# A causal convolution, a Fourier mix and an MLP on one core: the order of GpSimd's preparations, and the shape and order of the first input transfers

## The chip, the cores and the metric

The kernel runs on one core of a Trainium2 chip. A core has five instruction queues that run beside each other and wait for one another by semaphores: TensorE (PE, matrix products into PSUM), VectorE (DVE), ScalarE (ACT), GpSimd (POOL) and SyncE (SP), which here only issues DMAs. Each queue works through its instructions in order. Sixteen DMA engines move data between the off-chip memory (DRAM) and the on-chip memory (SBUF). The metric is the time of one execution on the device in microseconds, lower is better.

## What is computed

For 8 sequences of 4224 tokens with 192 features, in float32:

```python
# x: (8, 4224, 192), weight: (8 heads, 7 taps), group = 24 features a head
w = softmax(weight, axis=-1)
x = sum over k of w[h, k] * x_padded[b, s + k, head h]     # causal, 7 taps
X = np.fft.fft(np.fft.fft(x, axis=1), axis=2)               # over tokens, then features
u = x + np.real(X)
un = (u - mean(u)) / sqrt(var(u) + 1e-6)                    # over the features
out = u + np.maximum(un @ w_ch1, 0) @ w_ch2                 # 192 -> 768 -> 192
```

## The kernel before

**Per sequence (a "batch").** The convolution is a product with a band matrix (`conv_unit`, L419), in 6 chunks of 6 windows of 120 rows; its result is stored to a scratch `sc` in DRAM (`store_rows`, L383 and L391), with the first 1080 rows stored a second time behind the last, so that reads may run past the end. The transform over 4224 = 128 x 33 tokens starts from the scratch: partition a, column b of the input holds row 33a + 128b (modulo 4224). This input comes as 33 columns in eight pieces of four or five (`PIECES`), and each piece is split into two halves of 16 bits: `XH` by ScalarE (L530) and `XL` by VectorE (L538). `stage_a` (L555 to L564) transforms over a, `stage_b` (L581 to L592) over b, and the rest is done tile by tile.

**Per tile.** A batch has nine tiles ("steps", 72 in all): eight of 512 tokens and one of 128. For each, `load_res` fetches the convolution's rows from the scratch into `u`: two of the four groups by direct transfers from SP (L621), two by an indirect gather from GpSimd (L627). `prep` finishes the transform on PE (L678), adds it to `u` on VectorE (L696), takes mean and variance there (`mv`, L703 and L704), and then, for all tiles but the very first, works on GpSimd: a chain of six small instructions for the inverse root (`v`, `y`, `t`, L723 to L728), the normalised tile `un` (L732, four instructions), its upper 16-bit half (L746) and its lower half in two instructions (L749). The last of these is noted in the dictionary `lows` under the tile's number. `transposes` (L763) turns `hl` into `kt` with a DMA transpose from SP; `mlp_hidden` (PE L792, ACT L796 for `hh`, VectorE L797 for `hlo`) and `mlp_out` (PE L811 to L817, VectorE L823) follow, and SP stores the result.

**The order of the work.** A loop over n = 0 to 72 traces the work of several tiles interleaved: the MLP of tile n with the output of n - 1, `un` and the halves of tile n + 2 (`rest`), `prep` up to `y` of tile n + 3 (`sums`), the gathers of tile n + 5, and the convolution, input and transforms of later batches as filling. The instructions' order in each engine's queue is then chosen at build time by a scheduler with a model of the times. `tc.issue_after(ins)`, and `after(ins)` which does nothing where `ins` is missing, bind that order: what is traced in the block stands behind `ins` in the queue of `ins`'s engine. It adds an order and no wait. The second batch's input pieces (`load_x`, L489) are bound behind the transpose traced last (`turn[0]`), and share four buffers.

**The very first input.** Batch 0 has no filling before it. `load_first_x` loads its input into the two buffers that later hold `yh` and `yl`, in four ranges of columns, (0, 9), (9, 17), (17, 25) and (25, 33). Each range is loaded in four transfers of 32 partitions (L515). `WRAP` gives, for each 32 partitions, the column from which the row number passes 4224. Behind the last transfer SP loads the constants (`c16`), the taps, and the second batch's windows and rows. The gathers of tiles 0 to 3 have no `lows` to stand behind.

Of the kernel before, what the change touches and what calls it, by code (L numbers as in the profile page):

```python
# [11 lines left out]
F32 = mybir.dt.float32  # L12
# [3 lines left out]
ALU = mybir.AluOpType  # L16
# [3 lines left out]
B, S, D, HID = 8, 4224, 192, 768  # L20
# [7 lines left out]
NA, NB, NJ, ND = 128, 33, 64, 3  # L28
# [6 lines left out]
AC = 32  # L35
WRAP = (33, 25, 17, 9)
# [17 lines left out]
LNEPS = 1e-6  # L54
# [72 lines left out]
def kernel(  # L127
# [13 lines left out]
    nc = tc.nc  # L141
    PSUM = bass.MemoryType.PSUM
    cp = ctx.enter_context(tc.tile_pool(name="cp", bufs=1))
    sb = ctx.enter_context(tc.tile_pool(name="sb", bufs=2))
# [63 lines left out]
    def after(ins):  # L208
        return tc.issue_after(ins) if ins else ExitStack()
# [283 lines left out]
    def load_first_x(bt):  # L493

        halves = [
            sb.tile([NA, 17, D], F32, tag=tag, name=f"xs_0_{tag}", bufs=1)
            for tag in ("yh", "yl")
        ]

        def rows_of(b0, b1):  # L500
            h, o = (halves[0], 0) if b0 < 17 else (halves[1], 17)
            return h[:, b0 - o : b1 - o]

        loads = []
        for b0, b1 in ((0, 9), (9, 17), (17, 25), (25, 33)):
            for ch in range(NA // AC):
                r = 33 * AC * ch + 128 * b0 - (S if b0 >= WRAP[ch] else 0)
                last = r + 33 * (AC - 1) + 128 * (b1 - 1 - b0)
                loads.append((b0, last, r, ch, b0, b1))
        for _, _, r, ch, b0, b1 in sorted(loads):  # L510
            src = bass.AP(
                bt.sc.tensor, bt.sc.offset + r * D,
                [[33 * D, AC], [128 * D, b1 - b0], [1, D]],
            )
            load = nc.sync.dma_start(rows_of(b0, b1)[AC * ch : AC * (ch + 1)], src)  # L515
        for i, piece in enumerate(PIECES):
            bt.xs[i] = rows_of(*piece)
        return load.ins

    def split_x(bt, i):  # L520
        b0, b1 = PIECES[i]
# [86 lines left out]
    def load_res(bt, it, g):  # L608

        b = bt.b  # L610
        if g == 0:
            bt.u[it] = sb.tile([128, 4, D], F32, tag="u", name=f"u_{b}_{it}", bufs=8)
        to = bt.u[it][:, g]

        def fetch(part, first, *dims):
            src = bass.AP(
                bt.sc.tensor,
                bt.sc.offset + first * D,
                [[step * D, n] for step, n in dims] + [[1, D]],
            )  # L620
            nc.sync.dma_start(part, src)  # L621

        if it == Q0 or g % 2:
            col = 0 if it == Q0 else 1 + 4 * it + g
            k = b * NIT + it
            with after(lows.get(k - 3, lows.get(k - 4))):
                nc.gpsimd.indirect_dma_start(  # L627
                    to, None, bt.sc[:S],
                    bass.IndirectOffsetOnAxis(ap=rows_sb[:, col : col + 1], axis=0),
                )  # L630
            return

        c0 = CG * it
        cs = -33 if g else 33

        def block(q0, q1, base):
            fetch(
                to[CG * (q0 - 1) : CG * (q1 - 1)],
                base + cs * c0 + 128 * q0, (128, q1 - q0), (cs, CG),
            )  # L640

        cut = 1
        while 128 * cut + min(cs * c0, cs * (c0 + CG - 1)) < 0:
            cut += 1
        if cut in (2, NQ - 1):
            cut += 1
        if cut > 1:
            block(1, cut, S)
        if cut < NQ:
            block(cut, NQ, 0)  # L650
        if it == 0 and g:
            fetch(to[0::CG], S // 2 + 128, (128, NQ - 1))

    def prep(bt, it):
# [47 lines left out]
        for g in range(ng):  # L702
# [5 lines left out]
        var = mv[:, :ng, 1]  # L708
        v, t, y = (
            sb.tile([128, 4], F32, tag=n, name=f"{n}_{b}_{it}", bufs=3)[:, :ng]  # L710
            for n in ("v", "t", "y")
        )
        if b + it == 0:
            V = nc.vector
            V.tensor_scalar(v, var, LNEPS, None, op0=ALU.add)
            nc.scalar.activation(y, v, AF.Sqrt)
            V.reciprocal(y, y)
            V.scalar_tensor_tensor(t, v, -0.5, y, op0=ALU.mult, op1=ALU.mult)
            V.tensor_tensor(t, t, y, op=ALU.mult)
            V.scalar_tensor_tensor(y, t, 1.5, y, op0=ALU.add, op1=ALU.mult)  # L720
        else:
            P = nc.gpsimd
            P.tensor_scalar(v, var, LNEPS, None, op0=ALU.add)  # L723
            P.tensor_tensor(y, v, minus_half[:, :ng], op=ALU.pow)
            P.tensor_tensor(t, y, y, op=ALU.mult)
            P.tensor_tensor(t, t, v, op=ALU.mult)
            P.tensor_scalar(t, t, -0.5, 1.5, op0=ALU.mult, op1=ALU.add)
            P.tensor_tensor(y, y, t, op=ALU.mult)  # L728
        yield
        un = sb.tile([128, 4, D], F32, tag="un", name=f"un_{b}_{it}", bufs=1)  # L730
        for g in range(ng):
            (nc.vector if b + it == 0 else nc.gpsimd).tensor_scalar(  # L732
                un[:, g], u[:, g], mv[:, g, 0:1], y[:, g : g + 1],
                op0=ALU.subtract, op1=ALU.mult,
# [167 lines left out]
    turn, lows = [None], {}  # L902
    first = batches[0]
# [25 lines left out]
    for ch in range(NCH):  # L929
        for part in range(3):  # L930
# [3 lines left out]
            )  # L934
    scales(first)
    last_load = load_first_x(first)
    with tc.issue_after(last_band), tc.issue_after(first.evicted):
        W1, s1 = weights_in()
# [75 lines left out]
    for n in range(len(steps) + 1):  # L1014
        bt, it = steps[n] if n < len(steps) else (None, 0)
# [93 lines left out]
```

## Time and profile before

| | us |
|---|---|
| median of 3 runs | 1238.72 |
| lowest, highest | 1238.15, 1240.5 |
| the profiled execution's own time | 1238.39 |
| its span, first to last instruction | 1236.6 |

| engine | busy us | share of the span |
|---|---|---|
| PE, matrix products | 1171.4 | 95% |
| PE, weight loads | 928.6 | 75% |
| VectorE | 818.3 | 66% |
| ScalarE | 595.6 | 48% |
| GpSimd | 768.3 | 62% |

The profile is one execution on the chip. In its rows, "L749" is a line of the kernel, the arrow in "hl<-un" leads from the tile that is read to the tile that is written, and the bracket at the end of a timeline row gives how long the engine sat idle before that row, and what ended it. SPq and ACTq are the queues of SP and ACT when they issue a DMA. The granted clock is the share of full speed at which TensorE was let run.

### The profile page before, as it was taken

What the parts mean: (1) busy time and instruction counts of PE and PEld (TensorE: products, weight loads), DVE (VectorE), ACT (ScalarE), POOL (GpSimd) and SP (SyncE); (2) the same over time, 40 slices, a digit from 0 to 9 for tenths busy, and PEclk for the clock granted to TensorE, in tenths of its full rate; (3) what the DMA queues carried; (4) which work ended last, traced back from release to release, by engine and by line L of the source; (5) the groups of instructions that cost most, each with busy time, mean ns of one, the idle gap of its engine ahead of it and who ended that gap; (6) DMA issues with size and microseconds to landing.
All of it is one profiled execution on the core that took longest, in us unless ns stands there. A gap on an engine that the chain in (4) does not pass through costs nothing.

```text
span 1236.6 us, 30122 instructions
## 1 busy us (share of the span) xinstructions
PE 1171.4 (95%) x12236; PEld 928.6 (75%) x12236; DVE 818.3 (66%) x1871; ACT 595.6 (48%) x983; POOL 768.3 (62%) x1103
## 2 busy tenths in 40 slices
PE   5289869999999999999999999999999999999998
PEld 4178657787878777787787878787687877787776
DVE  6777655687656975478656876468965687567543
ACT  5675545365544555446543565445454455333222
POOL 0207676479637785468854796467963688667840
PEclk9599989999999999999999999999999999999999
DMA  8964985566455756377645675557754643323321
GB/s 297 271 189 115 240 125 114 128 173 185 93 123 149 186 140 140 87 181 188 144 96 138 157 194 100 123 144 185 150 99 100 164 99 90 83 63 81 81 56 42
DMA packets 238506, 170.47 MB, mean 138 GB/s; under 512 B 119512, under 2 KB 222112, under 8 KB 238368
## 3 DMA queue, kind: packets, MB, share of 16 engines
q1 hardware_dynamic: 184888, 109.95, 38.9%
q10 hardware_dynamic: 46952, 45.24, 13.4%
q0 software_dynamic: 6528, 13.38, 4.4%
q8 instruction: 95, 1.56, 0.5%
q14 instruction: 43, 0.35, 0.1%
HBM read 83.82 MB, written 58.55 MB: 115 GB/s over the span
## 4 chain that ended last, share of the span: by engine, by line
PE 85%; DVE 7%; DMA 4%; ACT 1%; issue 1%; POOL 1%; SPq 1%; DVEq 0%; ACTq 0%; POOLq 0%
PE ph L792 32%; PE po L811 10%; PE po L817 10%; PE po L814 10%; PE pa L555 6%; PE pb L581 6%; PE pq L678 6%; PE pc L419 6%; DVE XL L538 1%; DMA xs<-sc 1%; DVE yl L564 1%; DVE hlo L797 1%; DVE u L696 1%; DMA xs_yh<-sc 1%; ACT XH L530 1%
## 5 line engine op out<-in xcount | busy, mean ns | idle before, releaser
L792 PE MATMUL ph<-kt,W 128*128 128x512 f16 (+1 forms) x2160 | 494.9, 362 | 8.6 <-DVE hlo L797 7.0
L797 DVE SCALAR_TENSOR_TENSOR hlo<-ph,hh 128x512 f16<-128x512 f32 (+1 forms) x400 | 271.3, 679 | 279.0 <-ACT hh L796 271.1
L796 ACT ACTIVATE hh<-ph 128x512 f16<-128x512 f32 (+1 forms) x400 | 237.0, 593 | 432.1 <-PE ph L792 422.0
L811 PE MATMUL po<-W,hh 128*128 128x192 f16 x1584 | 386.1, 246 | 9.6 <-ACT hh L796 9.6
L814 PE MATMUL po<-W,hh 128*128 128x192 f16 x1584 | 385.6, 246 | 0.0
L817 PE MATMUL po<-W,hlo 128*128 128x192 f16 x1584 | 384.6, 246 | 0.0
L792 PEld LDWEIGHTS <-W 128*128 128x128 f16 x2160 | 192.7, 98 | 149.3 <-issue 9.1
L732 POOL TENSOR_SCALAR un<-u,mv,y 128x192 f32<-128x192 f32 x260 | 270.4, 1046 | 6.5 <-POOL y L728 0.2
L627 POOL DMA_INDIRECT u<-sc,rows_sb x136 | 145.6, 1071 | 68.1 <-DMA xs_yh<-sc 37.2
L811 PEld LDWEIGHTS <-hh 128*128 128x128 f16 x1584 | 155.4, 98 | 27.2 <-ACT hh L796 10.2
L817 PEld LDWEIGHTS <-hlo 128*128 128x128 f16 x1584 | 154.8, 98 | 22.3 <-issue 0.8
L814 PEld LDWEIGHTS <-hh 128*128 128x128 f16 x1584 | 155.0, 98 | 16.8
L723 POOL TENSOR_SCALAR v<-mv 128x4 f32<-128x4 f32 (+1 forms) x71 | 24.5, 344 | 176.9 <-DVE mv L704 147.3
L419 PE MATMUL pc<-xt,band 128*120 128x144 f32 x724 | 113.0, 295 | 13.4 <-DMA band<-line_d 11.0
L749 POOL TENSOR_TENSOR hl<-un,hl 128x512 f16<-128x512 f32 (+2 forms) x142 | 121.2, 874 | 4.0
L419 PEld LDWEIGHTS pc<-xt,band 128*120 128x120 f32 x724 | 99.9, 188 | 19.9 <-issue 10.9
L538 DVE SCALAR_TENSOR_TENSOR XL<-xs,s_x,XH 128x768 f16<-128x768 f32 (+1 forms) x56 | 94.7, 1692 | 29.3 <-ACT XH L530 29.3
L601 POOL COPY V<-V 128x96 f16<-128x96 f16 x64 | 16.8, 264 | 151.3 <-DVE V L592 151.2
L696 DVE SCALAR_TENSOR_TENSOR u<-pq,g,u 128x128 f32<-128x128 f32 (+1 forms) x328 | 102.7, 378 | 12.1 <-PE pq L678 12.1
L563 ACT ACTIVATE yh<-pa 99x512 f16<-99x512 f32 x128 | 75.9, 598 | 66.1 <-PE pa L555 61.8
L555 PE MATMUL pa<-c_sb,XH 128*128 128x128 f16 x1024 | 102.1, 220 | 0.9 <-ACT XH L530 0.9
L530 ACT ACTIVATE XH<-xs,s_x 128x768 f16<-128x768 f32 (+1 forms) x56 | 93.6, 1683 | 17.3 <-DMA xs<-sc 17.3
(135 smaller groups left out, 1551.1 us busy)
## 6 DMA issues: line engine op xcount, KB each, us to landing
out_dram<-u SPq DMA_DIRECT2D x64, 384.0 KB
xt<-in_xw_dram ACTq DMA_DIRECT2D x30, 576.0 KB
sc<-xa ACTq DMA_DIRECT2D x30, 540.0 KB
xs<-sc SPq DMA_DIRECT2D x28, 288.0 KB
u<-sc SPq DMA_DIRECT2D x72, 96.0 KB
xt<-in_xw_dram SPq DMA_DIRECT2D x10, 576.0 KB
sc<-xa SPq DMA_DIRECT2D x10, 540.0 KB
xs<-sc SPq DMA_DIRECT2D x28, 192.0 KB
```

The lines of the kernel that those rows point to most:

```text
L419: nc.tensor.matmul(pc[:WR, h - h0], band[:, h, :WR], xt[:, :, h * GRP : (h + 1) * GRP], start=True, stop=True,)
L555: nc.tensor.matmul(pa[:, i], x[:, at], F[:, l], start=(n == 0), stop=(n == 2))
L627: nc.gpsimd.indirect_dma_start(to, None, bt.sc[:S], bass.IndirectOffsetOnAxis(ap=rows_sb[:, col : col + 1], axis=0),)
L696: nc.vector.scalar_tensor_tensor(to, src, bt.g, to, op0=ALU.mult, op1=ALU.add)
L732: (nc.vector if b + it == 0 else nc.gpsimd).tensor_scalar(un[:, g], u[:, g], mv[:, g, 0:1], y[:, g : g + 1], op0=ALU.subtract, op1=ALU.mult,)
L749: lower = (nc.vector if b + it == 0 else nc.gpsimd).tensor_tensor(bl[:, :, o : o + n], un[:, :ng, f], hi[:, :, f], op=ALU.subtract)
L792: nc.tensor.matmul(ph[:, n], W1[:, w, ht * 128 : (ht + 1) * 128], kt[:, k], start=(i == 0), stop=(i == len(order) - 1),)
L796: anchor[0] = nc.scalar.activation(hh, ph, AF.Relu).ins
L797: nc.vector.scalar_tensor_tensor(hlo, ph, 0.0, hh, op0=ALU.max, op1=ALU.subtract)
L811: nc.tensor.matmul(po[:, g % 2], hh[:, ht, tk], W2[:, ht, 0], start=(ht == 0), stop=False)
L814: nc.tensor.matmul(po[:, g % 2], hh[:, ht, tk], W2[:, ht, 1], start=False, stop=False)
L817: nc.tensor.matmul(po[:, g % 2], hlo[:, ht, tk], W2[:, ht, 0], start=False, stop=(ht == 5),)
```

## The change

There are three edits. In `prep`, the first GpSimd instruction of a tile is bound behind the lower halves of the last tile whose halves have been traced. In `load_first_x`, each of the four column ranges is loaded in one transfer, or in two where the row numbers wrap inside it (one below the wrap, one above), seven in all; each is bound behind the one before. A new small GpSimd copy reads four elements of column 32 in all partitions, which the last transfers write, and the gathers that have no earlier tile to stand behind (tiles 0 to 3) are bound behind that copy.

```diff
 def load_first_x(bt):
-        loads = []
+        load = None
         for b0, b1 in ((0, 9), (9, 17), (17, 25), (25, 33)):
-            for ch in range(NA // AC):
-                r = 33 * AC * ch + 128 * b0 - (S if b0 >= WRAP[ch] else 0)
-                last = r + 33 * (AC - 1) + 128 * (b1 - 1 - b0)
-                loads.append((b0, last, r, ch, b0, b1))
-        for _, _, r, ch, b0, b1 in sorted(loads):
-            src = bass.AP(
-                bt.sc.tensor, bt.sc.offset + r * D,
-                [[33 * D, AC], [128 * D, b1 - b0], [1, D]],
-            )
-            load = nc.sync.dma_start(rows_of(b0, b1)[AC * ch : AC * (ch + 1)], src)
+            cut = next(c for c in range(5) if c == 4 or b0 >= WRAP[c])
+            for c0, c1, wrap in ((0, cut, 0), (cut, 4, S)):
+                if c0 == c1:
+                    continue
+                src = bass.AP(
+                    bt.sc.tensor,
+                    bt.sc.offset + (33 * AC * c0 + 128 * b0 - wrap) * D,
+                    [[33 * D, AC * (c1 - c0)], [128 * D, b1 - b0], [1, D]],
+                )
+                with after(load):
+                    load = nc.sync.dma_start(
+                        rows_of(b0, b1)[AC * c0 : AC * c1], src
+                    ).ins
         for i, piece in enumerate(PIECES):
             bt.xs[i] = rows_of(*piece)
-        return load.ins
+        landed = sb.tile([128, 4], F32, tag="v", name="landed", bufs=3)
+        bt.landed = nc.gpsimd.tensor_copy(landed, halves[1][:, 15, :4]).ins
+        return load
...
 def load_res(bt, it, g):
-            with after(lows.get(k - 3, lows.get(k - 4))):
+            with after(lows.get(k - 3, lows.get(k - 4, first.landed))):
                 nc.gpsimd.indirect_dma_start(
...
 def prep(bt, it):
             P = nc.gpsimd
-            P.tensor_scalar(v, var, LNEPS, None, op0=ALU.add)
+            with after(lows[max(lows)] if lows else None):
+                P.tensor_scalar(v, var, LNEPS, None, op0=ALU.add)
             P.tensor_tensor(y, v, minus_half[:, :ng], op=ALU.pow)
```

## The prediction

> **What bounds the kernel now.** I read the page first, for where TensorE (PE) is not full, then a table of busy time by stage, then PE's waits, then the queues behind the longest wait.
>
> ```profile
> span 1236.6 us, 30122 instructions
> ...
> PE   5289869999999999999999999999999999999998
> ```
>
> Each digit is the busy tenth of 30.9 us. From the seventh slice on PE is full; whatever the change does to time, it does in the first six slices, or in a hole too short for a digit. The table by stage gives the columns PE, PE's weight loads, VectorE (DVE), ScalarE (ACT) and GpSimd (POOL), then granted clock, DMA share and GB/s.
>
> ```profile
> 124.00:155.00 31.00, 26.63 (x239) 20.49 (x238) 19.03 (x41) 16.93 (x21) 19.26 (x26) 1.00 0.92 237
> 155.00:186.00 31.00, 20.56 (x206) 15.68 (x204) 16.48 (x27) 13.02 (x21) 21.96 (x24) 0.83 0.82 124
> 500.00:840.00 340.00, 340.00 (x3615) 272.99 (x3614) 227.19 (x523) 168.69 (x279) 219.68 (x317) 1.00 0.59 142
> 840.00:900.00 60.00, 56.45 (x556) 42.54 (x553) 51.47 (x105) 32.54 (x50) 52.18 (x67) 0.97 0.78 167
> ```
>
> From 500 to 840 PE is busy for all of 340 us: nothing that GpSimd does better there can be seen. Between 124 and 186 it lacks 4.4 and 10.4 us, and around 870 another 3.6. PE's waits between 60 and 190 us (total, times, longest) name the places:
>
> ```profile
> PE po L811 <- ACT hh L796: 9.6, 3, 8.7
> PE ph L792 <- DVE hlo L797: 2.9, 3, 1.1
> PE pc L419 <- ACT xa L428: 2.4, 1, 2.4
> PE ph L792 <- DMA kt<-hl: 1.7, 1, 1.7
> ```
>
> One wait of 8.7 us, for an activation, outweighs the rest. Four finer stretches around it:
>
> ```profile
> 154.00:158.00 4.00, 2.95 (x27) 2.21 (x25) 4.00 (x8) 3.74 (x6) 3.60 (x3) 1.00 0.02 4
> 158.00:162.50 4.50, 4.50 (x37) 3.04 (x35) 1.98 (x4) 0.61 (x2) 4.00 (x5) 1.00 0.59 119
> 162.50:171.25 8.75, 0.05 (x2) 0.01 (x1) 0.51 (x1) 2.13 (x3) 8.41 (x13) 0.75 1.09 225
> 171.25:177.10 5.85, 5.16 (x28) 3.35 (x29) 4.20 (x5) 2.53 (x3) 5.75 (x5) 0.50 1.17 119
> ```
>
> From 162.5 to 171.25 PE stands still, and in the next 5.85 us it has half its clock: 5.16 us of work there would be 2.6 at full clock. And from 154 to 158 the DMA engines did nothing (share 0.02), just ahead of the stretch in which everything waits for a load. GpSimd's timeline says why:
>
> ```profile
> 145.26 0.82 POOL L746 CAST hl<-un 128x768 f16<-128x768 f32 x1
> 146.07 0.19 POOL L727 TENSOR_SCALAR t<-t 128x4 f32<-128x4 f32 x1
> 154.32 1.41 POOL L723 TENSOR_SCALAR v<-mv 128x4 f32<-128x4 f32 x1 [8.05 <-DVE mv L704]
> 155.81 2.94 POOL L749 TENSOR_TENSOR hl<-un,hl 128x512 f16<-128x512 f32 x2
> ```
>
> The upper half of one tile was cast by 146.1. Its lower half (L749) needs nothing more, but it is queued behind L723, the first instruction of a later tile, and that waits 8.05 us for VectorE's variance. The lower half ends at 158.75; then SyncE (SP), ACT and the transfer follow:
>
> ```profile
> 158.78 3.66 SPq L763 DMA_TRANSPOSE kt<-hl  x1
> 162.53 2.94 SPq L489 DMA_DIRECT2D xs<-sc  x4
> ```
>
> ```profile
> 164.04 5.00 DMA xs<-sc
> ```
>
> ```profile
> 169.12 1.59 ACT L530 ACTIVATE XH<-xs,s_x 128x768 f16<-128x768 f32 x1 [10.35 <-DMA xs<-sc]
> ```
>
> The transpose waits for the lower half, the second batch's last two input pieces are queued behind the transpose, one of them lands 5.00 us after its issue, and ACT sits 10.35 us in front of it, with the hh that PE wants behind that. This chain is what the GpSimd part of the change cuts.
>
> **Part one: L723 behind the lower halves of the tile ahead.** No instruction is added; an order is. What is now queued behind the waiting L723 is the later tile's own chain, the gathers and the V copies; all of these stood behind it before too. What leaves from behind it is L746 and L749.
>
> Step by step: L749 can start at 146.1 and takes 1.8 us undisturbed (below, 850.00), so the transpose is issued near 148.0 instead of 158.78, 10.8 us sooner. The four row transfers then come up near 151.7 (its 3.66 us of issue after it), if their buffers are free. A buffer is freed by the VectorE split of the piece four earlier:
>
> ```profile
> 147.21 1.56 DVE L538 SCALAR_TENSOR_TENSOR XL<-xs,s_x,XH 128x768 f16<-128x768 f32 x1 [2.31 <-ACT XH L530]
> ...
> 151.87 1.55 DVE L538 SCALAR_TENSOR_TENSOR XL<-xs,s_x,XH 128x768 f16<-128x768 f32 x1
> ```
>
> These end at 148.8 and 153.4, so the sixth piece is bound by SP, the seventh by the buffer. With the 1.5 us from first to second transfer and 5.00 to landing, the pieces land near 158.3 and 159.5, in the stretch whose DMA share is 0.02 now. ACT's wait of 10.35 us ended at 169.12, so ACT has other work until 158.8 and the wait goes nearly whole, hh follows near 161, and PE, which stopped at 162.5, does not stop. That takes out 8.7 us, and with it the 2.6 us lost at half clock: the half clock follows the stand-still. The 1.7 us for kt is the same mechanism two tiles earlier, L723 waiting in front of L749, and goes too. Sum 13.0.
>
> What is late next: the loads now fall into a time with more DMA traffic, and the two splits (1.59 us in the row above) come earlier among ACT's and VectorE's work for the MLP. I give back 1.5 us for this, one split's length. The waits for hlo (2.9) I leave standing: they come from 1.6 us splits standing between two hlo on the same engine, which the change leaves. Part one: **-11.5 us** there.
>
> The third hole has the same form, smaller:
>
> ```profile
> 849.68 0.23 POOL L723 TENSOR_SCALAR v<-mv 128x4 f32<-128x4 f32 x1 [2.13 <-DVE mv L704]
> 850.00 1.80 POOL L749 TENSOR_TENSOR hl<-un,hl 128x512 f16<-128x512 f32 x2
> ```
>
> ```profile
> 866.61 2.29 PE L792 MATMUL ph<-kt,W 128*128 128x512 f16 x5 [3.07 <-DVE hlo L797]
> ```
>
> L749 is held 2.1 us, and the transpose, the last pieces and the segment load for the final batch follow it on SP; VectorE waits for that load with hlo behind. I credit the 2.1 us that L749 is held, out of a hole of 3.07 plus about 1 us of half clock. **-2.1 us**; bounds 0 and 4.1.
>
> Everywhere else PE is full, so the new order is worth nothing, and costs nothing while GpSimd has idle time to put it in.
>
> **Part two: the first transform input.** Sixteen transfers of 32 partitions become seven of 32 to 128, in fixed order; the eight gathers of the first four tiles move behind a new 128x4 copy that waits for the last of them. The copy itself is a quarter of a microsecond on an engine that has nothing else to do (L723, the same shape, takes 0.23).
>
> ```profile
> 45.54 6.54 ACT L530 ACTIVATE XH<-xs_yh,s_x 128x768 f16<-128x768 f32 x4 [4.45 <-DMA xs_yh<-sc]
> 51.96 6.15 ACT L530 ACTIVATE XH<-xs_yl,s_x 128x768 f16<-128x768 f32 x4
> ```
>
> ```profile
> 37.62 1.27 POOL L627 DMA_INDIRECT u<-sc,rows_sb  x1 [37.19 <-DMA xs_yh<-sc]
> ```
>
> The eight ScalarE splits run back to back from 45.54 to 58.11, so this stage is set by when the *first* piece is whole, not by the last. That piece now lies in four narrow transfers, and narrow transfers of later pieces stand between them in SP's queue. After the change it is the first transfer alone. Its price: it reads nearly all rows of the scratch, so it waits for the last store. The gather, which reads all of it, started at 37.62, so the scratch was whole by then at the latest. For the speed I compare the narrow loads with a stretch that holds wide ones:
>
> ```profile
> 37.00:43.00 6.00, 0.59 (x2) 0.50 (x2) 3.41 (x11) 2.12 (x5) 4.29 (x4) 0.50 1.14 204
> 384.50:388.00 3.50, 3.50 (x38) 3.00 (x36) 3.50 (x12) 0.60 (x1) 0.26 (x1) 1.00 1.11 329
> ```
>
> ```profile
> 382.27 3.03 SPq L489 DMA_DIRECT2D xs<-sc  x6
> ```
>
> Both have a full DMA share; 204 GB/s against 329 for the same 768-byte rows out of the same scratch. The first transfer is 9 x 128 rows of 768 bytes, 0.885 MB: 2.7 us at 329, and 2.5 us more from issue to flow (a 0.295 MB load took 5.00 in a crowd). Landing: 37.6 + 5.2 = 42.8, against 45.5 now. All 3.24 MB take 9.9 us, so the last lands near 50.0; the last pieces' splits would start near 52, so ACT stays unbroken. Gain 2.7, and since 37.6 is the latest for the stores, I take **-3 us**. Bounds: 0 (narrow speed: 4.3 us instead of 2.7 for the first piece, and 15.9 for all, hence the last at 56, which eats the gain at the other end) and 4.2 (stores whole 1.5 us before the gather). Behind this stage the split, stage A and the first tiles follow in a chain, so the gain stays on the path.
>
> [...]
>
> The gathers start near 50.3 instead of 37.6, and then take their eight issues. The first tile wants its rows here:
>
> ```profile
> 75.96 1.55 DVE L696 SCALAR_TENSOR_TENSOR u<-pq,g,u 128x192 f32<-128x192 f32 x5 [1.74 <-PE pq L678]
> ```
>
> Even 3 us sooner, that is 23 us after 50.3, for two gathers of a microsecond or so each; hidden. SP comes to what is queued behind the loads (c16, the second batch's windows) after seven issues; six take 3.03 us in the row at 382.27, so no later than now.
>
> **Sum** against the profiled execution's own 1238.39 us (span 1236.6): 1238.4 - 11.5 - 2.1 - 3.0 = 1221.8. The median of the runs shown is 1238.72, 0.3 higher; I say **1222**. About 0.2% (2.5 us) is what a measurement of this kernel can tell from no change.
>
> **Rivals.**
> Forecast, 1214 to 1229: chance 0.50.
> *One, width pays nothing:* stage A starts when it did, part one stays: 1238.4 - 13.6 = 1225. For it: the share is full in both rows, so the narrow loads are not starved of work. Against: 204 and 329. 0.15.
> *Two, the wait moves:* the last pieces land no sooner than buffers and a crowded DMA allow (share 0.92 from 124 to 155), ACT still stands in front of them for half as long, and PE stops for over 3 us, so that the half clock stays: half of 8.7 back, and 2.6. 1221.8 + 7 = 1229, to 1233. Against: the share of 0.02 between 154 and 158. 0.15.
> *Three, the change doesn't do what it says:* the order of L723 is right, but another waiting instruction (a V copy, a gather) comes to stand before L749, and only the start pays, or not that: 1235 to 1238. The instructions' order is chosen anew at build time. 0.10.
> *Four, slower:* GpSimd becomes the bound. Before, a later tile's y chain (L723 to L728) filled the gaps of the tile ahead; now tiles go one after another:
>
> ```profile
> 839.95 0.24 POOL L723 TENSOR_SCALAR v<-mv 128x4 f32<-128x4 f32 x1 [3.49 <-DVE mv L704]
> ...
> 842.56 4.00 POOL L732 TENSOR_SCALAR un<-u,mv,y 128x192 f32<-128x192 f32 x4
> ```
>
> From v to un 2.6 us, un 4.0, with the rows above cast 0.8, halves 1.8 and two gathers 2.5: 11.7 us a tile.
>
> ```profile
> L723 POOL TENSOR_SCALAR v<-mv x71: 234/239/1409, 92.8 to 1189.5; 128x4 f32<-128x4 f32 x63, 128x1 f32<-128x1 f32 x8
> ```
>
> 71 of these in 1096.7 us are one in 15.7 us. It decides from a pace under 11.7 us; if every tile lost 0.5 us to it, 70 tiles are 35, so about 1257. Against: POOL is busy for 219.68 of 340 us. 0.10 with all else that is slower.
>
> **How the numbers follow.** Low: full removal of the middle holes (13.0 and the 2.9 for hlo), 4.1 and 4.2 are 24.2, and 2 us for shorter holes: 1212. High: rival two's end, 1233, and one more for the start: 1234. Left out: rival three's far half, four. Faster by over 0.2%: 0.50 + 0.15 + 0.15 + 0.05 = 0.85; the same: 0.05, the other half of rival three; slower 0.10.
>
> **What would show it.** In the changed trace L749 should follow its L746 with no L723 between, and no idle time; the transpose near 159 should come over 10 us sooner, no ACT wait of 10 us for xs should stand, and PE's clock should hold 1.0 from 155 to 186. At the start the first XH split should begin near 42.8, the gathers after 50, and the stretch of the loads should move over 300 GB/s. Wrong would be: a first split after 45 (width), a new wait of PE for hh or kt of over 3 us (rival two), POOL without idle time in the full stretch (rival four).

## The result, and the profile after

The median is 1230.97 us of five runs (1226.93 to 1231.36), against 1238.72 us before (five runs, 1236.77 to 1240.5): a ratio of 0.9926, 95% interval 0.9904 to 0.9948 (taken over all the runs; the two medians alone would give 0.9937). The kernel is faster by 7.7 us, inside the stated range, and not by the 17 us that were forecast. The profiled execution of the changed kernel took 1231.06 us, with a span of 1228.8.

Most line numbers have moved: L723 is now L729, L746 L752, L749 L755, L763 L769, L831 L837, L530 L535, L534 L539, L555 L560, L563 L568, L590 L595, L627 L632, L792 L798, L796 L802, L797 L803, L811 L817.

From the page of the changed kernel: the span, each engine's busy time, and PE's busy tenths of 30.7 us.

```profile
span 1228.8 us, 30112 instructions
...
PE 1174.9 (96%) x12236; PEld 932.5 (76%) x12236; DVE 816.0 (66%) x1871; ACT 594.7 (48%) x983; POOL 785.0 (64%) x1104
...
PE   5379999999999999999999999998999999999998
```

The third slice has a 7 where the kernel before had an 8, and the fifth and sixth have 9s where it had 8 and 6. Time was gained in one place and lost in another. The table by stage of the changed kernel (PE, PE's weight loads, VectorE, ScalarE, GpSimd, clock, DMA share, GB/s):

```profile
124.00:155.00 31.00, 30.97 (x273) 23.85 (x271) 21.00 (x49) 18.48 (x27) 27.74 (x40) 1.00 1.02 235
155.00:186.00 31.00, 29.35 (x326) 23.47 (x325) 26.59 (x52) 20.84 (x32) 27.66 (x31) 1.00 0.69 156
840.00:900.00 60.00, 56.89 (x539) 43.54 (x537) 47.83 (x95) 32.34 (x53) 53.70 (x65) 0.97 0.74 156
```

PE now lacks 0.03 and 1.65 us where it lacked 4.4 and 10.4, at full clock. The stretch at 840 is nearly as it was (56.45 busy, 0.97). GpSimd's timeline shows why the first two rows filled:

```profile
146.40 0.82 POOL L752 CAST hl<-un 128x768 f16<-128x768 f32 x1
147.31 1.79 POOL L755 TENSOR_TENSOR hl<-un,hl 128x512 f16<-128x512 f32 x2
```

The halves follow their cast, with no v between them. PE's waits from 60 to 190 us hold no hh or kt any more, and one wait for hlo where there were 2.9 us in three:

```profile
PE pa L560 <- issue: 3.5, 5, 1.3
...
PE ph L798 <- DVE hlo L803: 1.7, 1, 1.7
```

The first of these rows is new, and it lies at the other place. ScalarE's timeline of the changed kernel, from the first input to stage A:

```profile
41.84 3.54 ACT L535 ACTIVATE XH<-xs_yh,s_x 128x768 f16<-128x768 f32 x2 [0.82 <-DMA xs_yh<-sc]
45.54 3.25 ACT L535 ACTIVATE XH<-xs_yh,s_x 128x768 f16<-128x768 f32 x2 [0.17 <-DMA xs_yh<-sc]
49.47 3.12 ACT L535 ACTIVATE XH<-xs_yl,s_x 128x768 f16<-128x768 f32 x2 [0.67 <-DMA xs_yl<-sc]
53.31 3.12 ACT L535 ACTIVATE XH<-xs_yl,s_x 128x768 f16<-128x768 f32 x2 [0.73 <-DMA u<-sc]
60.00 0.60 ACT L568 ACTIVATE yh<-pa 99x512 f16<-99x512 f32 x1 [3.57 <-issue]
60.81 0.60 ACT L568 ACTIVATE yh<-pa 99x512 f16<-99x512 f32 x1 [0.21 <-issue]
67.23 2.06 ACT L568 ACTIVATE yh<-pa 99x512 f16<-99x512 f32 x4 [5.82 <-remote]
```

The first split begins 3.7 us sooner than before (45.54), but the splits come in pairs with waits between, and stage A starts only half a microsecond sooner. Then ScalarE stands for 5.82 us inside stage A, and what it waited for the profile can't name. It isn't alone. The table by stage for that place, again of the changed kernel:

```profile
61.00:68.00 7.00, 3.29 (x40) 2.38 (x38) 1.22 (x3) 1.18 (x3) 3.13 (x4) 0.94 1.06 316
68.00:74.00 6.00, 5.40 (x52) 5.40 (x52) 4.42 (x7) 3.16 (x7) 0.00 (x0) 0.50 0.44 111
```

For 7 us PE, VectorE and ScalarE are each idle for more than half of the time, and PE pays with 6 us at half clock. The kernel before is busy on PE for all of these 7 us, at a DMA share of 0.97 and 307 GB/s. Whatever this stall is, it costs about as much as is missing from the forecast.

To see where each kernel gains and loses, all traces are cut at the same two instructions of ScalarE: its first copy of V, where stage B begins, and a split of the third batch. In the kernel before they are these rows of its timeline:

```profile
72.61 0.97 ACT L590 ACTIVATE V<-pb 128x408 f16<-128x408 f32 x2 [1.66 <-PE pb L581]
...
266.91 1.65 ACT L530 ACTIVATE XH<-xs,s_x 128x768 f16<-128x768 f32 x1
```

In the changed kernel they start at 80.36 and 258.83. So the first part of the span (up to the V copy) became 7.75 us longer, the middle 15.83 shorter (194.30 to 178.47), and the rest, up to the end of the span, 0.28 longer. The table below gives these three differences for every run; they come from one profiled execution each, whose span is in the last column. The medians and ratios are over 4 to 12 runs, against 5 to 24 runs of the kernel before, whose medians were 1238.72 to 1239.43.

| kernel | median us | ratio, 95% interval | start | middle | rest | span |
|---|---|---|---|---|---|---|
| changed kernel, first measurement | 1230.97 | 0.9926 (0.9904 to 0.9948) | +7.75 | -15.83 | +0.28 | 1228.8 |
| changed kernel again | 1224.10 | 0.9899 (0.9862 to 0.9935) | +0.56 | -18.02 | +0.56 | 1219.7 |
| GpSimd order alone | 1226.47 | 0.9891 (0.9871 to 0.9911) | +0.10 | -17.56 | +1.56 | 1220.7 |
| loads and held gathers alone | 1240.64 | 1.0008 (0.9996 to 1.0019) | +0.10 | +2.35 | -1.15 | 1237.9 |
| changed, gathers free | 1233.28 | 0.9931 (0.9904 to 0.9959) | +2.35 | -16.43 | +4.78 | 1227.3 |
| changed, narrow loads | 1224.00 | 0.9870 (0.9850 to 0.9891) | -0.40 | -17.04 | -0.76 | 1218.4 |
| changed, other warm-up | 1239.07 | 0.9999 (0.9979 to 1.0019) | -1.17 | +4.58 | -0.21 | 1239.8 |
| narrow loads in range order | 1240.34 | 1.0011 (0.9993 to 1.0029) | -1.49 | -1.43 | -0.68 | 1233.0 |
| the same, other warm-up | 1228.27 | 0.9907 (0.9881 to 0.9933) | -2.21 | -10.27 | -0.62 | 1223.5 |
| range order, store bound | 1234.49 | 0.9964 (0.9945 to 0.9983) | +5.13 | -12.78 | +3.55 | 1232.5 |
| wide, other warm-up, store bound | 1231.56 | 0.9948 (0.9922 to 0.9974) | +5.06 | -11.26 | -1.10 | 1229.3 |
| range order, other warm-up, store bound | 1229.32 | 0.9921 (0.9893 to 0.9949) | +7.74 | -16.61 | -1.43 | 1226.3 |
| kernel before, store bound | 1228.07 | 0.9908 (0.9889 to 0.9927) | +1.10 | -10.77 | -0.03 | 1226.9 |

### The profile page after: what moved, and what is told of

It is laid out like the page before. It is cut to its first block, busy times and chain, and to the rows that moved or that the text cites. A ratio compares the mean times of both kernels' runs of the same rounds, so it can differ in the third digit from the quotient of the medians.

```text
span 1228.8 us, 30112 instructions
## 1 busy us (share of the span) xinstructions
PE 1174.9 (96%) x12236; PEld 932.5 (76%) x12236; DVE 816.0 (66%) x1871; ACT 594.7 (48%) x983; POOL 785.0 (64%) x1104
## 3 DMA queue, kind: packets, MB, share of 16 engines
q8 instruction: 95, 1.56, 0.5%
## 4 chain that ended last, share of the span: by engine, by line
PE 85%; DMA 7%; DVE 4%; SPq 1%; issue 1%; ACT 1%; another core or an unknown queue 0%; DVEq 0%; ACTq 0%
PE ph L798 32%; PE po L817 10%; PE po L823 10%; PE po L820 10%; PE pa L560 7%; PE pb L586 6%; PE pc L419 6%; PE pq L683 5%; DMA xt<-in_xw_dram 3%; DMA xs<-sc 1%; ACT XH L535 1%; DMA xg<-in_xg_dram 1%; DMA raw_w1c<-in_w_dram 1%; DVE XL L543 1%; SPq L516 1%
## 5 line engine op out<-in xcount | busy, mean ns | idle before, releaser
L798 PE MATMUL ph<-kt,W 128*128 128x512 f16 (+1 forms) x2160 | 493.8, 362 | 5.6 <-DVE hlo L803 5.6
L803 DVE SCALAR_TENSOR_TENSOR hlo<-ph,hh 128x512 f16<-128x512 f32 (+1 forms) x400 | 271.6, 679 | 277.2 <-ACT hh L802 259.8
L802 ACT ACTIVATE hh<-ph 128x512 f16<-128x512 f32 (+1 forms) x400 | 236.8, 592 | 421.0 <-PE ph L798 397.7
L817 PE MATMUL po<-W,hh 128*128 128x192 f16 x1584 | 385.5, 246 | 0.0
L798 PEld LDWEIGHTS <-W 128*128 128x128 f16 x2160 | 192.6, 98 | 145.4 <-issue 6.8
L738 POOL TENSOR_SCALAR un<-u,mv,y 128x192 f32<-128x192 f32 x260 | 283.9, 1098 | 7.8
L817 PEld LDWEIGHTS <-hh 128*128 128x128 f16 x1584 | 155.2, 98 | 17.0 <-issue 0.3
L632 POOL DMA_INDIRECT u<-sc,rows_sb x136 | 146.4, 1077 | 31.5 <-issue 30.3
L755 POOL TENSOR_TENSOR hl<-un,hl 128x512 f16<-128x512 f32 (+2 forms) x142 | 125.6, 906 | 5.7
L568 ACT ACTIVATE yh<-pa 99x512 f16<-99x512 f32 x128 | 75.6, 598 | 79.7 <-PE pa L560 61.5
L606 POOL COPY V<-V 128x96 f16<-128x96 f16 x64 | 19.5, 307 | 143.2 <-DVE V L597 143.1
L569 DVE SCALAR_TENSOR_TENSOR yl<-pa,yh 99x512 f16<-99x512 f32 x128 | 86.2, 684 | 36.0 <-ACT yh L568 35.0
L560 PE MATMUL pa<-c_sb,XH 128*128 128x128 f16 x1024 | 106.0, 224 | 1.9 <-issue 1.1
L543 DVE SCALAR_TENSOR_TENSOR XL<-xs,s_x,XH 128x768 f16<-128x768 f32 (+1 forms) x56 | 92.0, 1642 | 16.4 <-ACT XH L535 12.8
L829 DVE SCALAR_TENSOR_TENSOR u<-po,fo,u 128x384 f32<-128x384 f32 (+1 forms) x136 | 81.1, 596 | 30.7 <-PE po L823 30.5
```

The lines of the kernel that those rows point to most:

```text
L543: nc.vector.scalar_tensor_tensor(part(XL), src, bt.c, part(XH), op0=ALU.mult, op1=ALU.subtract)
L560: nc.tensor.matmul(pa[:, i], x[:, at], F[:, l], start=(n == 0), stop=(n == 2))
L632: nc.gpsimd.indirect_dma_start(to, None, bt.sc[:S], bass.IndirectOffsetOnAxis(ap=rows_sb[:, col : col + 1], axis=0),)
L738: (nc.vector if b + it == 0 else nc.gpsimd).tensor_scalar(un[:, g], u[:, g], mv[:, g, 0:1], y[:, g : g + 1], op0=ALU.subtract, op1=ALU.mult,)
L755: lower = (nc.vector if b + it == 0 else nc.gpsimd).tensor_tensor(bl[:, :, o : o + n], un[:, :ng, f], hi[:, :, f], op=ALU.subtract)
L798: nc.tensor.matmul(ph[:, n], W1[:, w, ht * 128 : (ht + 1) * 128], kt[:, k], start=(i == 0), stop=(i == len(order) - 1),)
```

## The experiments

**The two parts apart.** The theory after the result was that the held gathers, which now run beside stage A, starve it. The rival was that the wide loads cost the time, or that part one gives less than its trace shows. Four kernels share the runs of the kernel before.

Part one alone:

```diff
-            P.tensor_scalar(v, var, LNEPS, None, op0=ALU.add)
+            with after(lows[max(lows)] if lows else None):
+                P.tensor_scalar(v, var, LNEPS, None, op0=ALU.add)
```

> The change's first part alone: L723's v waits behind the halves of the tile ahead; the first transform's loads are the sixteen narrow ones and the gathers are free, as before the change. Theory (the order on GpSimd is worth some 15 us, and the wide loads with held gathers cost some 8 of them back at the start of stage B): 1222 to 1225 us, the first matmul of pb near 71.0 us as before the change, and no 8.7 us stand-still of TensorE before 186 us. Rival (the order gives only the whole difference that was seen, and the loads neither give nor take): 1230 to 1232 us.

Measured 1226.47 us, between the two expectations and nearer to the theory's; the profiled execution, with 1222.55, has the theory's size. The middle is 17.56 us shorter; stage B starts when it did.

Part two alone, that is, the changed kernel with the line of part one as it was before:

> The change's second part alone: seven wide loads, the landed copy and gathers behind it; GpSimd's preparations are free to start as before the change. Theory (the loads and held gathers cost some 8 us at the start of stage B): 1243 to 1248 us with the first matmul of pb near 78.8 us; should the stand-still of TensorE at 150 us swallow some of it, 1239 to 1243. Rival (the second part gives 0 to 3 us as forecast, and the first part was overrated): 1235 to 1238 us with the first matmul of pb before 71 us.

Measured 1240.64 us, a ratio of 1.0008: no difference that can be measured. As a number it lies in the theory's second range, but the mark of that range, a first matmul of pb near 78.8 us, is not there (71.10), so neither expectation came true. The V copy is 0.10 us late, with the gathers beside stage A and no stall. So the gathers' place alone doesn't make the stall.

The changed kernel with free gathers (wide loads kept):

```diff
-            with after(lows.get(k - 3, lows.get(k - 4, first.landed))):
+            with after(lows.get(k - 3, lows.get(k - 4))):
```

> The changed kernel with its wide loads, but the gathers of tiles 0 to 3 wait for nothing. Theory (the held gathers run beside stage A and cost the 8 us there): 1219 to 1224 us, gathers issued from about 37 us, the first matmul of pb near 70 us. Rival one (the wide loads themselves, with the idle time of ScalarE between their splits, cost it): 1229 to 1232 us with the first matmul of pb near 78 us. Rival two (neither is the cause, the stall at 61 us belongs to something else that moved): 1229 to 1232 us with the stall in stage A still there.

Measured 1233.28 us, above all three expectations; the first matmul of pb is at 73.35 us, neither at 70 nor at 78. There is no stall in stage A of this trace, but the loads now share the DMA engines with the gathers and the last pair of splits begins at 56.21 instead of 53.31; stage B starts 2.35 us late. Another 4.78 us are lost in the rest, where this wasn't followed up.

The changed kernel with the sixteen narrow loads, gathers held behind them. Against the kernel before, beside the two edits with `after` in `load_res` and `prep`, it adds:

```diff
         for i, piece in enumerate(PIECES):
             bt.xs[i] = rows_of(*piece)
+        landed = sb.tile([128, 4], F32, tag="v", name="landed", bufs=3)
+        bt.landed = nc.gpsimd.tensor_copy(landed, halves[1][:, 15, :4]).ins
         return load.ins
```

> The changed kernel with the sixteen narrow loads of before, and the gathers of tiles 0 to 3 held behind the last of them. Theory (held gathers beside stage A cost the 8 us, and wide loads give 1 to 3): 1230 to 1235 us, first matmul of pb at 78 us or later. Rival (the wide loads cost it): 1221 to 1225 us, first matmul of pb at 69 to 71 us.

Measured 1224.00 us, the lowest median of the study and the rival's number, with the first matmul of pb at 70.61 us: the gathers may be held, and the wide loads bring nothing that can be measured. Its ScalarE timeline (L532 and L565 are L535 and L568 of the changed kernel) shows the difference:

```profile
45.15 6.53 ACT L532 ACTIVATE XH<-xs_yh,s_x 128x768 f16<-128x768 f32 x4 [4.38 <-DMA xs_yh<-sc]
51.58 6.14 ACT L532 ACTIVATE XH<-xs_yl,s_x 128x768 f16<-128x768 f32 x4
60.13 10.42 ACT L565 ACTIVATE yh<-pa 99x512 f16<-99x512 f32 x16 [2.41 <-PE pa L557]
```

It begins its splits 3.3 us later, works through them without a wait, and comes to stage A 0.13 us behind the changed kernel.

**Is the stall part of the change?** The changed kernel was run once more, unaltered.

> The changed kernel itself once more, for the 5.8 us in which ScalarE, VectorE and TensorE stood together from 61.4 us on (stage A) in its first trace. If the stall belongs to the change, it is there again and the first V copy is near 80 us (80.36). If it is an event of that one execution, stage A runs through as in the trace with the second part alone, the first V copy is at 72 to 75 us, and the profiled execution takes 1223 to 1227 us.

The median of seven runs was 1224.10 us, and the profiled execution took 1221.86, a microsecond less than the lower expectation. ScalarE's timeline of it:

```profile
50.05 3.13 ACT L535 ACTIVATE XH<-xs_yl,s_x 128x768 f16<-128x768 f32 x2 [0.47 <-DMA xs_yl<-sc]
54.10 3.13 ACT L535 ACTIVATE XH<-xs_yl,s_x 128x768 f16<-128x768 f32 x2 [0.92 <-DMA xs_yl<-sc]
60.80 0.60 ACT L568 ACTIVATE yh<-pa 99x512 f16<-99x512 f32 x1 [3.57 <-PE pa L560]
61.64 9.86 ACT L568 ACTIVATE yh<-pa 99x512 f16<-99x512 f32 x15 [0.25 <-PE pa L560]
```

Fifteen copies in a row: no stall. The stall comes in some executions of this program and not in others. The twelve times of the changed kernel agree with that: seven from 1221.8 to 1227.2 and five from 1231.0 to 1234.5, with nothing between, and the two profiled ones, 9.2 us apart, fall one in each group. Only those two have a trace, so for the other ten the stall is inferred from the time alone.

**What does the width do?** Two kernels. The first has other warm-up products ahead of stage A, since the pairs of splits leave a hole in the warm-up. From PE's timeline of the changed kernel:

```profile
51.12 2.96 PE L539 MATMUL idle<-W,XH 128*12 128x512 f16 x6 [12.59 <-ACT XH L535]
54.97 2.96 PE L539 MATMUL idle<-W,XH 128*12 128x512 f16 x6 [0.89 <-ACT XH L535]
57.87 1.03 PE L560 MATMUL pa<-c_sb,XH 128*128 128x128 f16 x8
```

and from that of the kernel before:

```profile
53.62 4.29 PE L534 MATMUL idle<-W,XH 128*12 128x512 f16 x9 [15.02 <-ACT XH L530]
58.17 0.63 PE L555 MATMUL pa<-c_sb,XH 128*128 128x128 f16 x8 [0.26 <-ACT XH L530]
```

Before, the warm-up ran through and the first eight products of stage A took 0.63 us; now it has a hole of 0.89 us, and they take 1.03.

```diff
-        if bt.b == 0 and i > 3:
+        if bt.b == 0 and 1 < i < 7:
...
-            for w in range(3):
+            for w in range(12 if i == 5 else 4):
```

> The changed kernel with other warm-up products ahead of stage A: four each behind splits 2, 3, 4 and 6, twelve behind split 5, none behind split 7, where there were three each behind splits 4 to 7 (their result is read by nothing). Theory (the wide loads let ScalarE's splits come in pairs, so that TensorE's warm-up has a hole, and stage A and then the first convolution products run at half clock): the clock is full from 56 us, yh starts near 58.5 us, no half clock at 74 to 77 us, 1221 to 1225 us. Rival (the clock is not it): 1229 to 1232 us with the half clock gone.

The second has the narrow loads in the wide ones' order. Shown against the narrow loads of the kernel before; all else is as in the changed kernel:

```diff
-            load = nc.sync.dma_start(rows_of(b0, b1)[AC * ch : AC * (ch + 1)], src)
+            with after(load):
+                load = nc.sync.dma_start(
+                    rows_of(b0, b1)[AC * ch : AC * (ch + 1)], src
+                ).ins
```

> The changed kernel with sixteen narrow loads again, but bound in the order of the column ranges, each behind the one before, so that only their width differs from the wide ones. Rival one of the prediction (width pays nothing): the first split begins at 41 to 43 us and the last load lands at 52 to 54 us, the same as with the wide loads, and the splits come in groups with waits between; then the time is that of the changed kernel, 1227 to 1232 us. If width pays, the first split begins over 1 us later and the last load lands over 2 us later than with the wide ones. If the wide shape is what costs, 1221 to 1225 us, the time with the narrow loads in the old order.

At the start both did nearly what was expected. With the other warm-up the clock is full from 54 us and yh starts at 59.35 instead of 60.00 or 60.80. With narrow loads in range order the first split begins at 40.97, sooner than with any of the wide ones (41.84 to 43.13), and stage A at 59.04. From 41 us on the speed of the loads is nearly the same: two stretches of the kernel with part two alone (wide),

```profile
41.00:45.00 4.00, 0.00 (x0) 0.00 (x0) 0.92 (x2) 1.87 (x2) 0.00 (x0) 0.50 1.14 230
45.00:49.00 4.00, 0.00 (x0) 0.00 (x0) 3.68 (x3) 3.74 (x3) 0.00 (x0) 0.50 1.14 204
```

and of the narrow loads in range order:

```profile
41.00:45.00 4.00, 0.00 (x0) 0.00 (x0) 2.17 (x3) 4.00 (x3) 0.00 (x0) 0.50 1.15 205
45.00:49.00 4.00, 0.00 (x0) 0.00 (x0) 4.00 (x4) 3.85 (x4) 0.00 (x0) 0.50 1.14 194
```

Before that it is not. While the first wide load runs, the second trace of the changed kernel has

```profile
39.00:40.00 1.00, 0.00 (x0) 0.00 (x0) 0.48 (x3) 0.78 (x2) 0.00 (x0) 0.50 1.06 353
40.00:41.00 1.00, 0.00 (x0) 0.00 (x0) 0.97 (x2) 0.66 (x1) 0.00 (x0) 0.50 1.10 351
```

and the narrow loads in range order have

```profile
39.00:40.00 1.00, 0.00 (x0) 0.00 (x0) 0.32 (x3) 0.00 (x0) 0.00 (x0) 0.50 1.18 184
40.00:41.00 1.00, 0.00 (x0) 0.00 (x0) 0.00 (x0) 0.03 (x1) 0.00 (x0) 0.50 1.00 184
```

But the narrow loads start sooner: the first is issued at 33.03 us, the first wide one, which reads what more of the stores wrote, at 36.30 to 36.95. The order of the ranges alone brings the first split forward, without the width. Why the wide loads behind the first are slower, and whether the first owes its speed to its width or to having few loads beside it, no run shows.

But both whole kernels took 1239 to 1240 us, as if part one weren't there: both expectations missed. The loss is in the middle. SP's queue of the narrow kernel in range order:

```profile
122.61 0.37 SPq L837 DMA_DIRECT2D out_dram<-u  x1
123.08 1.64 SPq L769 DMA_TRANSPOSE kt<-hl  x1
...
145.15 0.36 SPq L837 DMA_DIRECT2D out_dram<-u  x1
145.61 1.64 SPq L769 DMA_TRANSPOSE kt<-hl  x1
```

and the halves for these two transposes on GpSimd:

```profile
114.40 1.78 POOL L755 TENSOR_TENSOR hl<-un,hl 128x512 f16<-128x512 f32 x2
126.75 1.78 POOL L755 TENSOR_TENSOR hl<-un,hl 128x512 f16<-128x512 f32 x2
```

The halves were ready at 116.18 and 128.53; the transposes went out 6.9 and 17.1 us later, each right behind the store of an older tile's result, which waits for VectorE (14.6 and 6.3 us among SP's waits from 100 to 150 us). GpSimd's order was the right one. The kernel with the other warm-up has the same order on SP: halves ready at 118.90 and 131.29, transposes at 124.27 and 148.94, and PE waits 10.6 us for kt. An edit at the start made the build-time scheduler draw SP's order differently, and that took the place of the wait which part one removes: PE waits 4.2 us for hh and 4.8 for hlo in the narrow kernel.

**The other warm-up with narrow loads in range order:**

> The kernel with sixteen narrow loads in the order of the column ranges, with the other warm-up products (four behind splits 2, 3, 4 and 6, twelve behind split 5). Clock theory: 1220 to 1224 us, first matmul of pb at 68.5 to 70 us. If the hole in the warm-up does not matter: as with the narrow loads in range order alone.

Measured 1228.27 us. The start is the best of all, 2.21 us ahead of the kernel before. SP's order came out right at 113 us, and yet the middle gains 10.27 us, not 17. PE's waits there are for kt, 4.3 us in two, so it came out above the clock theory's 1220 to 1224 us. One transpose whose halves were ready at 140.49 is issued at 148.26, behind eight input loads and a store.

**SP's order bound as well.** To test what was read from SP's queue, the store is bound behind the transpose traced last, in three of the kernels and in the kernel before:

```diff
-            if it == Q0:
-                nc.sync.dma_start(out0[b], u[:, 0])
-            else:
-                nc.sync.dma_start(out1[b, it].rearrange("p (g d) -> p g d", g=4), u)
+            with tc.issue_after(turn[0]):
+                if it == Q0:
+                    nc.sync.dma_start(out0[b], u[:, 0])
+                else:
+                    nc.sync.dma_start(
+                        out1[b, it].rearrange("p (g d) -> p g d", g=4), u
+                    )
```

> Narrow loads in the order of the column ranges, as one run before, with one order more: the store of a tile's result (L837) is bound behind the transpose traced last. In the trace of one run before, SP had that store at 122.6 us ahead of a transpose whose halves were ready at 116.2, and another at 145.2 ahead of one ready at 140.5. Theory (that order on SP, drawn anew by the build-time scheduler, is what cost 16 us, not the loads): 1219 to 1226 us, transposes at 116 and 128 to 129 us, no wait of TensorE for hh or kt over 2 us between 95 and 186 us. Rival (stage A's earlier start or the order of the loads costs it): 1236 to 1242 us.

(The second transpose named there was read wrongly: its halves were ready at 128.5, as above.) Measured 1234.49 us, between the two expectations and 5.9 below the same kernel without the binding, with intervals that don't meet. SP's queue in the same place:

```profile
121.95 1.42 SPq L769 DMA_TRANSPOSE kt<-hl  x1
...
134.72 2.53 SPq L769 DMA_TRANSPOSE kt<-hl  x1
```

Their halves ended at 121.92 and 134.69. The wait for hh is gone, and the middle gains 12.78 us where it gained 1.43. That the time is still above what was expected has two reasons in the table: the stall of stage A is in this execution (yh starts 2.3 us ahead of the kernel before, V 5.13 behind), and the rest is 3.55 longer.

> Wide loads with the other warm-up products, as in the earlier run, and the result's store bound behind the transpose traced last. Theory (the order on SP cost it): 1219 to 1226 us, with transposes issued as soon as their halves are there. Rival (the warm-up products cost it): 1236 to 1242 us.

Measured 1231.56 us, again between the two expectations, against 1239.07 without the binding; the middle goes from +4.58 to -11.26. The stall is there too (yh ahead by 1.3, V behind by 5.06).

> Narrow loads in range order, the other warm-up products, and the result's store bound behind the transpose traced last: the candidate for the best. If the store's order still costs something in this kernel (its transposes already stood ahead of the stores at 116 and 128 us): 1216 to 1221 us. If what is left is the first transposes' transfers in a crowd, it stays: 1225 to 1229 us.

Measured 1229.32 us, no better than without the binding, so not the best version, and just above the second expectation, whose reason was wrong: the waits for kt are gone and the middle is now 16.61 shorter instead of 10.27. In the profiled execution the stall took that back (yh ahead by 1.6, V behind by 7.74).

> The kernel before with nothing but the result's store bound behind the transpose traced last; its GpSimd order isn't bound, but the scheduler now draws the lower halves ahead of the later tile's v in the one tile that mattered (the cast at 145.26). If the orders of that one place, on GpSimd and on SP, are the whole of part one: 1221 to 1227 us. If the binding on GpSimd does something that this doesn't: 1232 to 1239 us.

Measured 1228.07 us, 1 us above the first expectation. One order on SP, and not a word to GpSimd, gives 11 of the 13 us of part one alone, since the scheduler then draws the halves ahead of v in the tile that mattered. It is less than part one: the middle gains 10.77.

## Why the prediction was right and wrong

The sign and the mechanism of part one were right, and all three terms were mis-sized: part one too small, the other two too large. For an execution without the stall the sum came out (1222 forecast, 1221.86 profiled and a median of 1224.10 the second time), but by luck: in that trace -18.0, +0.6 and +0.6 stand where -11.5, -2.1 and -3.0 were forecast, and the errors cancel. The 9 us between the forecast and the first median are mostly the stall, for which the prediction had no term; from the start of yh to the V copy that trace takes 8.3 us longer than the kernel before.

**Part one: -11.5 forecast; -15.8 to -18.0 in the middle in the four traces that have the order and the same order on SP with the old warm-up, -16.4 with free gathers.** What was to be seen was seen: halves directly behind the cast, the transpose that went out at 158.78 out at 154.43 in the slower start and at 144.76 in the second trace, full clock from 155 to 186. The size was off because only the longest waits were taken out. The second trace of the changed kernel, by stage:

```profile
124.00:155.00 31.00, 30.27 (x273) 23.63 (x271) 24.56 (x47) 20.86 (x28) 28.48 (x33) 1.00 1.08 256
155.00:186.00 31.00, 31.00 (x379) 25.66 (x377) 23.28 (x43) 20.41 (x34) 24.68 (x32) 1.00 0.58 133
```

PE lacks 0.73 us of 62, against 14.8 before. 14.1 of idle time and the 2.6 at half clock make 16.7; the middle shows 18.0. The prediction quoted the 4.4 and 10.4 and then counted 8.7 and 1.7 of them. The waits for hlo, left standing, shrank too (2.9 to 0.7 us in this trace), and nothing was given back where 1.5 was set aside. The step that failed is the choice to price the named waits and not the stage.

**The hole at 866: -2.1 forecast, none.** The rest of the span is 0.28 and 0.56 longer in the two traces of the changed kernel, and it is shorter by 1.15 in the kernel with part two alone, where the order on GpSimd is free. L749 is no longer held there, but VectorE waits as long as before for the last batch's segment load `xg` (3.67 and 3.10 us in the two traces, 3.32 before), and PE stands as long for hlo (3.11 and 2.94 us, 3.07 before). So the step that failed is the link from L749 to that load; what holds the load wasn't tested.

**Part two: -3.0 forecast; +0.1 to +0.6 at the V copy where there was no stall.** Three steps failed. *The speed*: 329 GB/s held for the first load alone (353 and 351 in the rows above), and the first split came at 41.84 to 43.13 where 42.8 was forecast. The loads behind it moved at 204 to 230, the narrow ones at 194 to 205, and the last pair of splits began at 53.31 to 54.10 where near 52 was forecast. Rival one was right about them: wide or narrow, they moved at nearly the same speed. The 2.5 us from issue to flow were the author's estimate; in the first trace of the changed kernel the first load is issued at 36.30 us, the DMA share is 0.43 from 37 to 38 and 0.88 from 38 to 39, and the first split begins 5.5 us after the issue, where landing 5.2 us behind 37.6 was forecast. *"ACT stays unbroken"*: at the lower speed ScalarE is faster than the loads, and its splits wait in pairs (0.17 to 0.82 us ahead of each pair in the first trace). *What stands behind the splits* was not looked at: the warm-up products hang on them, and behind the hole in the warm-up the start of stage A ran at half clock (0.50 from 57 to 60 us and 0.83 from 60 to 61 in the first trace, against 0.70 from 57 to 58 and 1.00 from 58 on in the kernel before). The hole can't be the whole reason: in the narrow kernel in range order PE is busy for 1.50 of 2.00 us from 53 to 55, without and with the store bound, and the clock from 55 to 58 is 0.50 without and 1.00 with it. So a first split 2.4 to 3.7 us sooner (45.54 to 43.13 and 41.84) came to about half a microsecond at most (yh at 60.00 against 60.53). In the kernel with part two alone the clock falls once more, at the convolution behind the first V copy, in these rows by stage:

```profile
74.00:76.00 2.00, 2.00 (x27) 2.00 (x25) 0.33 (x1) 0.00 (x0) 0.26 (x1) 0.50 0.39 103
76.00:78.00 2.00, 2.00 (x20) 2.00 (x19) 0.34 (x2) 0.00 (x0) 0.00 (x0) 0.65 0.37 91
```

The kernel before does the same work there at full clock, and 0.50 of 2.00 and 0.35 of 2.00 make an estimated loss of 1.7 us:

```profile
74.00:76.00 2.00, 2.00 (x41) 2.00 (x38) 0.26 (x2) 0.00 (x0) 0.26 (x1) 1.00 0.40 95
```

This fall can't be put down to part two: the narrow loads in range order have it too (0.50 from 72 to 74 us), and so has the kernel before with the store bound (0.50 from 76 to 78), while the second trace of the changed kernel doesn't (1.00 from 70 to 80).

**The gathers, "hidden".** As transfers they are: where they were held and no stall came, the V copy moved by 0.10 us with part two alone and by -0.40 with the narrow loads. But all four traces with the stall (the first of the changed kernel, and the three kernels with held gathers and the store bound) have the eight held gathers beside stage A, and none of the four traces with free gathers has it, the kernel before among them. Six traces with held gathers don't have it either. So the held gathers may be a condition of the stall; they don't settle it, and its cause stays open. Nor do the untraced executions rule it out with free gathers: with the wide loads and free gathers, four of six took 1232.8 to 1235.0 us.

In all four, many landings (the records of a transfer's end) are missing at this place: the DMA view from 54 to 66 us gives no time to landing for the gathers in the first trace of the changed kernel,

```profile
u<-sc,rows_sb POOLq DMA_INDIRECT x8
```

and one in the second:

```profile
u<-sc,rows_sb POOLq DMA_INDIRECT x8, 6.8
```

Counted over all queues, 72 to 114 landing events are on record from 54 to 66 us where the stall is, and 194 to 237 where it isn't. The loss is not confined to that place. The four whole traces hold 9430 to 9824 landing events, nine of the other ten 10407 to 10585, and the tenth, the kernel before with the store bound, 9926, with free gathers and no stall. So lost records alone don't make the stall; in these fourteen traces it is there where records are lost and gathers are held, and nowhere else. The four kernels with the store bound were measured on one chip, which may be the reason for their loss; of the first trace of the changed kernel the chip isn't on record. Whether the stall comes from the chip, from the recording, or from something that also loses the records, no run here tells.

**Rival three** ("the instructions' order is chosen anew at build time") was given 0.10 for the change itself. It didn't happen to it, but something of its kind, on SP's queue, happened to two of the experiments, and there it took the whole gain. **Rivals two and four** didn't come, although the first median lies in rival two's 1229 to 1233: no new wait for hh or kt over 3 us, and GpSimd is busy for 785.0 of 1228.8 us.

## What to carry to other kernels

Where a stand-still is removed, price the whole stage by its missing busy time and clock, not by the waits that have a name: the short waits around it can come from the same lateness (here those for hlo, 2.9 us before and 0.7 in the second trace). Before a load is made earlier, look at what hangs on its consumers (here warm-up products; with others the clock was full from 54 us instead of 60 or 61) and don't take the speed of one load for that of a whole queue of them (353 and some 210 GB/s here). And where a build-time scheduler draws the queues, an edit at the start can redraw them far behind: compare the orders of every queue, SP's too, before the time of a variant is put down to its edit, and bind both ends of a chain that matters.

## What was not expected of the hardware

In one of two traces of one and the same program three engines stood together, ScalarE for 5.82 us at a stretch, with no releaser that the profile can name, and then PE ran 6 us at half clock. The DMA share was 1.06 at 316 GB/s; the other trace has 1.05 at 325 in the same 7 us, and PE busy throughout. In the four traces with the stall the way from the first yh to the V copy is 6.4 to 9.4 us longer, more than the 4.2 us that bounded part two. And the clock fell in one kernel and not in another after the same work: with part two alone and with the GpSimd order alone PE is busy for 1.06 of 2.00 us from 70 to 72 and for 1.40 from 72 to 74, and from 74 to 76 the clock is 0.50 in the first and 1.00 in the second. The clock had become full at about 60.3 us in the first of these two kernels and at about 58.3 in the second (estimates from rows of one microsecond, 0.84 from 60 to 61 and 0.86 from 58 to 59). Why it fell in the one alone, no run shows.
